# Gated mix of sliding-window attention and a gated GLU: the value product in 64-key halves per two query blocks

## The chip, the cores and the metric

One core of a Trainium2 chip runs the whole kernel. The metric is device time in microseconds (us) of one execution, as the median of several runs. A profiled execution gives, beside it, a trace of every instruction on the five engines: TensorE (PE, with its weight loads listed apart as PEld), VectorE (DVE), ScalarE (ACT), GpSimd (POOL) and SyncE (SP, which issues the DMAs).

## The reference

Both branches read the same input `x` of 2048 tokens by 512 features. The first is causal attention with 32 heads of 16 features and a window of 256 keys; the second is a GLU with 1376 hidden features; a sigmoid gate per token mixes them.

```python
q, k, v = split(x @ wqkv)                     # 32 heads of 16
mask = (i - j >= 0) & (i - j < 256)
p = softmax(where(mask, q @ k.T * 16**-0.5, -1e9))
a = (p @ v) @ wo
b = (sigmoid(x @ w_gate) * (x @ w_up)) @ w_down
g = sigmoid((x * gate_w).sum(-1))
out = g * a + (1 - g) * b
```

## The kernel before, in words

All tokens are cut into 16 blocks of 128, and the heads into 8 groups of 4. One pair of head group and block is a unit; there are 128 (`NU`), and a loop over `u` (lines 593 to 674) works through them with delays. In step `u` the kernel makes the scores of query block `u` with queries in the partitions (`s_part`, line 291), whose row maxima DVE takes (line 307). Nine steps later (`LAG`) it makes the scores again, transposed, with the keys of block `u - 9` in the partitions and up to 384 queries in the columns (`st_part`, line 339). ACT takes their exponential into a tile `pt` in SBUF (line 352) and POOL zeroes what the window excludes (`mask_p`, lines 357 and 362). Each of the two makes four tiles per step, one per head `hh`, in a pair of PSUM buffers of its own: tag `s` and tag `st`, two buffers each. A score matmul uses 64 of the 128 rows of the PE array, so one of `s` and one of `st` run side by side in the two row halves.

In every even step `pv_part` (line 371) multiplies the tiles `pt` of two units, `u - 12` and `u - 11`, with the value rows of their key block. Each head takes 32 columns of the array, so the four heads of a group run side by side on all 128 rows, and each writes 32 partitions of one PSUM bank, `pv`, that holds 512 queries. The products of the three key blocks that a query sees are added up in that bank over three units. As operands are fp32, every matmul is issued as two passes. After each second unit `o_take` (line 391) copies 256 finished queries to SBUF on ACT (line 396), and DVE then clears them in the bank (line 397). The 17th column of every head's value rows is 1, which gives the sums of the softmax.

Around this the PE is filled with projection work: "slots" (`run_slots`, line 573; `turns`, line 519), each with one matmul in either row half, of 512 columns, for the q and k projections (`pj`) and the GLU's gate and up products (`gu`), in three PSUM buffers of tag `misc`. In a step with both score kinds there are three slots behind each head's scores (line 644); in a step with a value product one of them is run right behind it, ahead of the first scores, and two behind these. In steps from 128 on there are no `s` scores, and six slots stand behind each second head. The order of all engines but POOL is the order of the program text; work that may wait is put in the lists `acts` (ACT) and `behind` (DVE), from which one entry is taken per head, and `later` (DMAs, issued at the start of the next step).

DMAs are issued by SP in program order. The row maxima go through DRAM into the tile `ring` (`max_store`, line 324, and `max_load`, line 330): those of query blocks 4s to 4s + 3 are stored at the start of step 4s + 4, loaded in step 4s + 5, and first used by `st_part` in step 4s + 7.

The value rows lie in SBUF in one tile `V` of 16 blocks by 560 floats, and the gate and up products, stored to DRAM, are loaded again into the same memory at the end (`h_load`, line 541): eight places, loads 0 to 4 in steps 130, 132, 134, 136 and 138 (line 669), the rest in the last loop (lines 732 to 782), which multiplies with `w_down` and `wo` in 128-row matmuls. The sigmoid of line 556 takes load 0 in step 138.

Of the kernel before, what the change touches and what calls it, by code (L numbers as in the profile page):

```python
# [7 lines left out]
F32 = mybir.dt.float32  # L8
# [21 lines left out]
VROW = H * VW + 16  # L30
# [17 lines left out]
def gated_mix_kernel(  # L48
# [28 lines left out]
    gu_d = nc.dram_tensor("gu_scratch", (2, NF, P, T), F32, kind="Internal").ap()  # L77
    max_d = nc.dram_tensor("max_scratch", (NG * NC, HG, 2, 4, P), F32, kind="Internal").ap()
# [39 lines left out]
    with ExitStack() as actx:  # L118
# [5 lines left out]
        V = apool.tile([P, NB, VROW], F32, name="V")  # L124
        Vh = V[:, :, 0:H * VW].rearrange("p b (h w) -> p b h w", w=VW)
# [22 lines left out]
        Vf = V.rearrange("p b v -> p (b v)")  # L148
        xraw = Vf[:, NB * VROW - 2 * ND * CH:].rearrange("p (c d t) -> p c d t", c=2, d=ND)
        wvraw = Vf[:, 0:ND * D].rearrange("p (d n) -> p d n", d=ND)  # L150
# [20 lines left out]
        for _ in range(14):  # L171
            mm(warm_ps[:, 0:2 * P], warm[:, 0:P], warm[:, 0:2 * P], start=True, stop=True)
        pv = ps.tile([P, CH], F32, tag="pv", name="pv", bufs=1)
        for k in range(2):
            mm(pv[:, 2 * P * k:2 * P * k + 2 * P], warm[:, 0:P], warm[:, 0:2 * P],
               start=k == 0, stop=True, skip_group_check=True)
# [32 lines left out]
        def fill_v(b0, b1):  # L209
            nc.gpsimd.memset(V[:, b0:b1, H * VW:], 0.0)  # L210
            nc.gpsimd.memset(Vh[:, b0:b1, :, DH:VW], 1.0)
# [5 lines left out]
        def v_part(b, d):  # L217
            if d == 0:
                vp[b] = ps.tile([P, D], F32, tag="misc", name=f"vps{b}", bufs=3)
# [119 lines left out]
        def st_part(u, hh):  # L339
            g, j = divmod(u, NB)  # L340
            if u not in pts:
                pts[u] = ppool.tile([P, HG, 3 * P], F32, tag="pt", name=f"pt{u}", bufs=3)
# [24 lines left out]
        later = []  # L367
        acts = []
        obs = {}

        def pv_part(u):
            g, j = divmod(u, NB)
            p = pts.pop(u)
            last = min(NB, j + 3)
            q = j
            while q < last:
                e = min(last, (q // 4 + 1) * 4)
                for hh in range(HG):
                    h = g * HG + hh
                    mm(  # L380
                        pv[32 * hh:32 * hh + 32, (q % 4) * P:(q % 4 + e - q) * P],
                        V[:, j, h * VW:h * VW + 32],
                        p[:, hh, (q - j) * P:(e - j) * P],
                        start=False, stop=True, skip_group_check=True,
                        tile_position=(0, 32 * hh),
                    )
                q = e
            if j % 2 == 1:
                acts.insert(0, lambda: o_take(g * NC + j // 4, j // 2 % 2))

        def o_take(s, half):
            g, c = divmod(s, NC)
            if half == 0:
                obs[s] = cpool.tile([P, CH], F32, tag="ob", name=f"ob{s}", bufs=2)
            cols = slice(2 * P * half, 2 * P * half + 2 * P)
            nc.scalar.copy(obs[s][:, cols], pv[:, cols])
            behind.insert(0, lambda: nc.vector.memset(pv[:, cols], 0.0))
            if half == 0:
                return
            ob = obs.pop(s)  # L400
# [61 lines left out]
        def gu_mm(f, c, w, k, half=None):  # L462
            fw = width(f, w)
            if (f, c, w) not in gp:
                gp[f, c, w] = ps.tile([P, CH], F32, tag="misc", name=f"gu{f}_{c}_{w}", bufs=3)
            group_mm(gp[f, c, w], fw, gv[:, 0, w, :, 0:fw], gv[:, 1, w, :, 0:fw], c, k, half)
# [72 lines left out]
        hv = Vf[:, 0:16 * CH].rearrange("p (n w t) -> p n w t", w=2, t=CH)  # L539

        def h_load(n):
            c, f = steps[n]
            for w in range(2):
                nc.sync.dma_start(hv[0:FCH[f], n % 8, w], gu_d[w, f, 0:FCH[f], c * CH:(c + 1) * CH])

        def h_skew(n):
            a, b = n + 2, n + 3
            if 0 <= a < len(steps):
                fw = FCH[steps[a][1]]
                hts[a] = cpool.tile([P, CH2], F32R, tag="hb", name=f"hb{a}", bufs=4)  # L550
                src = hv[0:fw, a % 8, 1]
                split(hts[a][0:fw, 0:CH], hts[a][0:fw, CH:], src)
            if 0 <= b < len(steps):
                fw = FCH[steps[b][1]]
                tg, tu = hv[0:fw, b % 8, 0], hv[0:fw, b % 8, 1]
# [31 lines left out]
        HLOAD = N - 2 * AHEAD  # L587
        WD = NU - 5
        done = 0
        slots = turns()  # L590
        sdma = []

        for u in range(N):
            if u == LAG:
                vctx.close()
                ppool = actx.enter_context(tc.tile_pool(name="ppool", bufs=1))
            if u == 4:
# [26 lines left out]
            for hh in range(HG):  # L624
                if hh == 0 and u % 2 == 0:
                    for w in (u - PVLAG - 1, u - PVLAG):
                        if 0 <= w < NU:
                            pv_part(w)
                head = u > PVLAG and hh == 0 and u % 2 == 0
                if head:  # L630
                    run_slots(1)
# [11 lines left out]
                if u >= LAG and (hh < HG - 1 or u % 2 == 0 if u < NU else hh % 2 == 1):  # L643
                    run_slots((GAP if u < NU else 2 * GAP) - (u > PVLAG and u % 2 == 0 and hh == (0 if u < NU else 1)))
# [24 lines left out]
            if u >= HLOAD and (u - HLOAD) % 2 == 0:  # L669
                h_load((u - HLOAD) // 2)  # L670
# [10 lines left out]
        assert not (work or first or going or behind or acts or raw_gu or sdma or pts or obs)  # L681
# [18 lines left out]
        spare = [ppool.tile([P, 3, CH], F32, tag="pt", name=f"spare{k}", bufs=3) for k in range(2)]  # L700
# [31 lines left out]
        for n, (c, f) in enumerate(steps):  # L732
# [39 lines left out]
            for t in range(4):  # L772
# [3 lines left out]
                pa = ps.tile([P, D], F32, tag="misc", name=f"pa{b}", bufs=3)  # L776
# [58 lines left out]
```

## Time and profile before

| | before |
|---|---|
| median of 3 runs | 759.92 us (757.31 to 761.72) |
| span of the profiled execution, first to last instruction | 756.7 us |
| PE busy, share of the span | 748.4 us, 99% |
| DVE, ACT, POOL busy | 480.4, 431.9, 165.8 us |
| matmuls | 6180 |

For the profiled execution itself the span is the time that is listed; it lies 3.2 us under the median of the runs, which also holds what lies around the first and the last instruction. Times inside the trace are us from the start of the span. A PE row gives a matmul's start and a modelled length; since matmuls are pipelined, the cost of one is read from start to next start.

### The profile page before, as it was taken

To read this page: it belongs to the slowest core of one execution; us is meant where nothing else is said; L and a number is where in the kernel's file an instruction comes from. 1 tells how busy PE (TensorE), PEld (TensorE's weight loads), DVE (VectorE), ACT (ScalarE), POOL (GpSimd) and SP (SyncE) were. 2 spreads that over 40 slices of the span, in tenths; PEclk is the share of its full clock that TensorE was granted. 3 is DMA by queue.
4 is the path that set the end of the run, shared out by engine and by line. 5 is a ranking of instruction groups with operands and counts; after the bars stand their busy time and mean duration, and the time that the engine had idled before them with its cause. 6 is when DMAs were issued, how large, how long until landed. Compare 5 with 4: busy or idle time off the path is not lost.

```text
span 756.7 us, 17519 instructions
## 1 busy us (share of the span) xinstructions
PE 748.4 (99%) x6180; PEld 575.8 (76%) x6180; DVE 480.4 (63%) x1459; ACT 431.9 (57%) x930; POOL 165.8 (22%) x256
## 2 busy tenths in 40 slices
PE   8999999999999999999999999999999999999997
PEld 6877777777777777787787777777766778888886
DVE  5346767776776766776677676677512785748381
ACT  5412666666676667666666666656665572616241
POOL 7000233233233233323323223332321000000000
PEclk9999999999999999999999999999999999999999
DMA  8340434426433453444543525443455966557351
GB/s 301 97 112 19 104 101 115 130 68 179 121 105 111 125 149 110 116 111 120 139 125 87 135 73 167 134 116 106 132 177 156 269 221 219 182 190 224 124 151 55
DMA packets 69959, 103.58 MB, mean 137 GB/s; under 512 B 19314, under 2 KB 29042, under 8 KB 69872
## 3 DMA queue, kind: packets, MB, share of 16 engines
q1 hardware_dynamic: 69872, 102.48, 46.0%
q8 instruction: 48, 0.79, 0.4%
q14 instruction: 39, 0.32, 0.2%
HBM read 45.26 MB, written 32.00 MB: 102 GB/s over the span
## 4 chain that ended last, share of the span: by engine, by line
PE 95%; DMA 3%; DVE 1%; ACT 1%; issue 0%; SPq 0%; DVEq 0%; ACTq 0%
PE gu L233 36%; PE pj L233 12%; PE pv L380 11%; PE st L347 6%; PE s L301 6%; PE pd L70 4%; PE pd L72 4%; PE pd L71 4%; PE vps L70 2%; DMA V<-gu_scratch 2%; PE vps L71 2%; PE vps L72 2%; PE pa L72 2%; PE pa L70 2%; PE pa L71 2%; DMA wdraw<-in_wd_dram 1%
## 5 line engine op out<-in xcount | busy, mean ns | idle before, releaser
L307 DVE CUSTOM_DVE_ANT_0 junk<-s,mask 128x384 f32<-128x384 f32 (+2 forms) x512 | 272.0, 531 | 146.8 <-PE st L347 66.4
L233 PE MATMUL gu<-xh,w 64*128 64x512 f32 (+3 forms) x1384 | 359.5, 397 | 0.0
L352 ACT ACTIVATE pt<-st 128x384 f32<-128x384 f32 (+2 forms) x512 | 243.5, 479 | 156.2 <-PE st L347 88.6
L233 PE MATMUL gu<-xl,w 64*128 64x512 f32 (+3 forms) x692 | 245.9, 397 | 0.0
L233 PEld LDWEIGHTS gu<-xh,w 64*128 64x128 f32 (+3 forms) x1384 | 204.5, 183 | 34.8 <-issue 10.5
L357 POOL TENSOR_SCALAR_AFFINE_SELECT pt<-pt 128x512 f32<-128x512 f32 x128 | 85.3, 666 | 392.1 <-ACT pt L352 392.1
L347 PE MATMUL st<-ring 64*128 64x384 f32 (+2 forms) x536 | 163.3, 317 | 0.0
L301 PE MATMUL s<-ring 64*128 64x384 f32 (+2 forms) x536 | 159.5, 320 | 0.0
L233 PEld LDWEIGHTS gu<-xl,w 64*128 64x128 f32 (+3 forms) x692 | 124.2, 183 | 13.2 <-issue 6.4
L347 PEld LDWEIGHTS st<-ring 64*128 64x128 f32 x536 | 97.2, 184 | 11.1 <-ACT pt L352 1.5
L301 PEld LDWEIGHTS s<-ring 64*128 64x128 f32 x536 | 94.8, 184 | 10.6 <-issue 2.9
L233 PE MATMUL pj<-xh,wqh 64*128 64x512 f32 (+1 forms) x232 | 95.4, 414 | 1.3 <-ACT xh L66 1.3
L233 PE MATMUL pj<-xl,wqh 64*128 64x512 f32 (+1 forms) x232 | 92.1, 400 | 0.0
L380 PE MATMUL pv<-pt,V 128*32 128x384 f32 (+2 forms) x1408 | 91.0, 388 | 0.0
L233 PE MATMUL pj<-xh,wql 64*128 64x512 f32 (+1 forms) x232 | 74.2, 398 | 0.0
L362 POOL TENSOR_SCALAR_AFFINE_SELECT pt<-pt 128x512 f32<-128x512 f32 x112 | 70.9, 633 | 0.0
L70 PE MATMUL pd<-ring,hb 128*128 128x512 f32 (+1 forms) x176 | 69.6, 395 | 1.3 <-ACT hb L66 1.3
L72 PE MATMUL pd<-ring,hb 128*128 128x512 f32 (+1 forms) x176 | 69.2, 393 | 0.2
L71 PE MATMUL pd<-ring,hb 128*128 128x512 f32 (+1 forms) x176 | 68.6, 390 | 0.4 <-DVE ring L111 0.4
L380 PEld LDWEIGHTS pv<-pt,V 128*32 128x32 f32 x1408 | 37.2, 109 | 35.9 <-issue 29.4
L471 ACT COPY sp<-gu 128x512 f32<-128x512 f32 (+2 forms) x88 | 51.4, 585 | 21.1 <-PE gu L233 19.7
L66 ACT CAST hb<-V 128x512 fp32r<-128x512 f32 (+1 forms) x44 | 27.3, 620 | 54.5 <-DVE V L557 54.2
(74 smaller groups left out, 904.4 us busy)
## 6 DMA issues: line engine op xcount, KB each, us to landing
gu_scratch<-sp SPq DMA_DIRECT2D x80, 256.0 KB
V<-gu_scratch SPq DMA_DIRECT2D x80, 256.0 KB
ring<-sh SPq DMA_DIRECT2D x128, 128.0 KB
ring<-sl SPq DMA_DIRECT2D x64, 128.0 KB
guraw<-in_wgu_dram SPq DMA_DIRECT2D x20, 256.0 KB
V<-in_xT_dram SPq DMA_DIRECT2D x16, 256.0 KB
oT_scratch<-ob SPq DMA_DIRECT2D x128, 32.0 KB
xl<-oT_scratch SPq DMA_DIRECT2D x16, 256.0 KB
```

The source lines that it names most:

```text
L70: mm(ps, lh, rh, start=first, stop=False)
L71: mm(ps, lh, rl, start=False, stop=False)
L72: mm(ps, ll, rh, start=False, stop=last)
L233: mm(pt[0:fw], (wl if w == 2 else wh)[r, d], (xl if w == 1 else xh)[r, d, c * CH:(c + 1) * CH], start=k == 0 and half != 1, stop=k == 3 * ...
L301: mm(pt[:, (k - k0) * P:(e - k0) * P], lhsT, blk(g, k, hh, 1, e - k), start=k == k0, stop=e == i + 1, skip_group_check=True,)
L307: nc.vector.tensor_tensor_reduce(junk[:, 0:n], pt[:, 0:n], mask[:, 3 * P - n:], scale=1.0, scalar=NEG, op0=ALU.add, op1=ALU.max, accum_out ...
L347: mm(pt[:, (q - j) * P:(e - j) * P], lhsT, blk(g, q, hh, 0, e - q), start=q == j, stop=e == last, skip_group_check=True,)
L352: nc.scalar.activation(pts[u][:, hh, 0:n], pt[:, 0:n], AF.Exp, scale=SCALE)
L357: nc.gpsimd.affine_select(p[:, :, 0:P], p[:, :, 0:P], pattern=[[0, HG], [1, P]], compare_op=ALU.is_ge, fill=0.0, base=0, channel_multiplie ...
L362: nc.gpsimd.affine_select(p[:, :, 2 * P:], p[:, :, 2 * P:], pattern=[[0, HG], [-1, P]], compare_op=ALU.is_gt, fill=0.0, base=0, channel_mu ...
L380: mm(pv[32 * hh:32 * hh + 32, (q % 4) * P:(q % 4 + e - q) * P], V[:, j, h * VW:h * VW + 32], p[:, hh, (q - j) * P:(e - j) * P], start=Fals ...
L471: nc.scalar.copy(t[0:width(f, w)], gp.pop((f, c, w))[0:width(f, w)])
```

## The change

The value product now goes by queries in place of keys. `pv_burst` computes, in the same even steps, the whole output of two query blocks `i` and `i + 1` of a head group at once, from the tiles `pt` of the key blocks `i - 2` to `i + 1`. Each key block is cut in two halves of 64 keys; one half is seen by 64 + 256 = 320 queries. The halves with even `k` run in the upper 64 rows of the array, those with odd `k` in the lower, each head in its 32 columns: eight tiles of 64 rows by 32 columns. Rows of the array that are apart must write different PSUM banks, so there are two sums, `acc[0]` and `acc[1]`, taken for the burst from the buffers of `s` and of `st`. `o_take` follows at once: ACT copies `acc[0]` to SBUF, DVE adds `acc[1]` to it. The bank `pv` and its clearing go; `misc` has four buffers.

A value row tile is no longer read in place. Every block of `V` is stored to DRAM (`v_d`) and the 68 columns of a head group are loaded from there as `vg` (`v_load`, one DMA of 16 x 128 rows of 272 bytes), at step 10 and then at steps 16, 32, ... The freed memory, `region`, holds seven tiles `pt`, and at the end seven places for `h_load`, whose loads 0 to 4 move to steps 135, 136, 137, 137 and 138.

```diff
-            if j % 2 == 1:
-                acts.insert(0, lambda: o_take(g * NC + j // 4, j // 2 % 2))
...
-            nc.scalar.copy(obs[s][:, cols], pv[:, cols])
-            behind.insert(0, lambda: nc.vector.memset(pv[:, cols], 0.0))
...
+        def v_load(g):
+            nc.sync.dma_start(
+                vg[g % 2][:, 0:NB * GW].rearrange("p (b w) -> p b w", w=GW),
+                v_d[:, :, g * GW:(g + 1) * GW].rearrange("b p w -> p b w"),
+            )
+
+        def pv_burst(u, n):
+            g, i = divmod(u, NB)
+            acc = [
+                ps.tile([P, CH], F32, tag=tag, name=f"pv{tag}{u}", bufs=2) for tag in ("s", "st")
+            ]
+            span = {
+                k: (max(0, 64 * k), min(n * P, 64 * k + 5 * 64))
+                for k in range(-4, 2 * n) if i + k // 2 >= 0
+            }
+            order = [
+                sorted((k for k in span if k % 2 == half), key=lambda k: (span[k][0] - span[k][1], k))
+                for half in range(2)
+            ]
+            for m in range(len(order[0])):
+                for hh in range(HG):
+                    for half in range(2):
+                        k = order[half][m]
+                        j = i + k // 2
+                        q0, q1 = span[k]
+                        o = -(k // 2) * P
+                        r = slice(64 * half, 64 * half + 64)
+                        c = j * GW + hh * VW
+                        mm(
+                            acc[half][32 * hh:32 * hh + 32, q0:q1],
+                            vg[g % 2][r, c:c + 32], pts[g * NB + j][r, hh, q0 + o:q1 + o],
+                            start=m == 0, stop=m == len(order[0]) - 1, skip_group_check=True,
+                            tile_position=(64 * half, 32 * hh),
+                        )
+            o_take(g, i, n, acc)
+
+        def o_take(g, i, n, acc):
...
+            nc.scalar.copy(part, acc[0][:, 0:n * P])
+            nc.vector.tensor_tensor(part[:, lo:], acc[1][:, lo:n * P], part[:, lo:], op=ALU.add)
...
-                pj[s] = ps.tile([P, CH], F32, tag="misc", name=f"pj{s}", bufs=3)
+                pj[s] = ps.tile([P, CH], F32, tag="misc", name=f"pj{s}", bufs=4)
...
+                later.append((v_d[b], V[:, b]))
...
-        HLOAD = N - 2 * AHEAD
+        HLOAD = {N - 5: [0], N - 4: [1], N - 3: [2, 3], N - 2: [4]}
...
+            if u == LAG + 1 or u % NB == 0 and 0 < u < NU:
+                v_load(u // NB)
...
-                    for w in (u - PVLAG - 1, u - PVLAG):
-                        if 0 <= w < NU:
-                            pv_part(w)
+                    if u in bursts:
+                        pv_burst(*bursts[u])
```

## Rows read from the trace of the kernel before

**Rows 1.** The page: busy time by engine, and the chain by engine.
```profile
PE 748.4 (99%) x6180; PEld 575.8 (76%) x6180; DVE 480.4 (63%) x1459; ACT 431.9 (57%) x930; POOL 165.8 (22%) x256
...
PE 95%; DMA 3%; DVE 1%; ACT 1%; issue 0%; SPq 0%; DVEq 0%; ACTq 0%
```

**Rows 2.** Timeline of PE, 304 to 307 us: start, length, line, out<-in, shape, count.
```profile
304.49 1.50 PE L380 MATMUL pv<-pt,V 128*32 128x384 f32 x16
305.92 0.50 PE L233 MATMUL pj<-xh,wqh 64*128 64x512 f32 x1
...
306.26 0.33 PE L347 MATMUL st<-ring 64*128 64x384 f32 x1
...
306.90 0.33 PE L347 MATMUL st<-ring 64*128 64x384 f32 x1
```

**Rows 3.** Timeline of PE, a value product of eight passes, at 312 us.
```profile
312.39 1.51 PE L380 MATMUL pv<-pt,V 128*32 128x256 f32 x32
313.83 0.50 PE L233 MATMUL gu<-xl,w 64*128 64x512 f32 x1
```

**Rows 4.** Groups by form: busy us, mean ns; idle before.
```profile
L307 DVE CUSTOM_DVE_ANT_0 junk<-s,mask 128x256 f32<-128x256 f32 x32 | 13.6, 425 | 14.6 <-PE st L347 10.5 <-PE s L301 3.7
```

**Rows 5.** Timeline of all engines around the last value product, 579 us.
```profile
578.28 0.86 PE L380 MATMUL pv<-pt,V 128*32 128x256 f32 x16
...
579.07 0.47 PE L233 MATMUL gu<-xh,w 128*96 128x512 f32 x1
...
579.25 0.37 ACT L396 COPY ob<-pv 128x256 f32<-128x256 f32 x1 [0.24 <-PE pv L380]
...
579.75 0.27 DVE L397 MEMSET pv<- 128x256 f32 x1 [4.02 <-ACT ob L396]
```

**Rows 6.** Timeline of all engines, 598 to 600.6 us.
```profile
598.51 0.62 ACT L66 CAST xh<-woraw 128x512 fp32r<-128x512 f32 x1 [5.76 <-DMA woraw<-in_wo_dram]
...
599.16 0.69 DVE L67 TENSOR_TENSOR xl<-woraw,xh 128x512 fp32r<-128x512 f32 x1 [1.00 <-ACT xh L66]
...
599.76 0.68 DVE L67 TENSOR_TENSOR hb<-V,hb 128x512 fp32r<-128x512 f32 x1
...
600.50 0.51 PE L72 MATMUL pd<-ring,hb 128*128 128x512 f32 x1
```

**Rows 7.** Timeline of PE around a late slot, 97 to 99 us.
```profile
97.72 0.33 PE L347 MATMUL st<-ring 64*128 64x384 f32 x1
...
98.00 0.49 PE L233 MATMUL gu<-xh,w 64*128 64x512 f32 x1
...
98.34 0.62 PE L233 MATMUL gu<-xh,w 64*128 64x512 f32 x2
```

**Rows 8.** Waits of PEld: us in total, times, longest.
```profile
PEld gu L233 <- ACT pr L245: 1.9, 6, 0.3
```

**Rows 9.** Timeline of PE, step 130.
```profile
548.65 0.37 PE L347 MATMUL st<-ring 64*128 64x384 f32 x2
```

**Rows 10.** Timeline of DVE at the start of the value product of rows 2.
```profile
304.42 0.08 DVE L307 DVE_READ_ACCUMULATOR2_ANT mx<- 128x1 f32 x1
```

**Rows 11.** Timelines of SP (step 16 on) and of PE (step 19).
```profile
103.37 1.70 SPq L328 DMA_DIRECT2D max_scratch<-nt  x4
...
108.56 0.56 SPq L333 DMA_DIRECT2D ring<-max_scratch  x1
...
114.37 0.34 PE L347 MATMUL st<-ring 64*128 64x384 f32 x1
```

**Rows 12.** The page: DMA queues (packets, MB, share of 16 engines).
```profile
q1 hardware_dynamic: 69872, 102.48, 46.0%
```

**Rows 13.** Timelines of SP (step 136) and of ACT (step 138).
```profile
572.49 0.82 SPq L544 DMA_DIRECT2D V<-gu_scratch  x2
...
580.94 0.63 ACT L556 ACTIVATE V<-V 128x512 f32<-128x512 f32 x1
```

More of the change, by code (lines that the diff above doesn't have):

```diff
@@ L29 @@
 VW = DH + 1
-VROW = H * VW + 16
+VROW = H * VW
+GW = HG * VW
+PR = 7
+PW = HG * 3 * P
+REGION = PR * PW
+NHV = 7
+HV0 = REGION - NHV * 2 * CH
+BURST = 2
 SCALE = DH ** -0.5
@@ L170, in gated_mix_kernel @@
         warm_ps = ps.tile([P, CH], F32, tag="st", name="warm_ps", bufs=2)
-        for _ in range(14):
+        for _ in range(16):
             mm(warm_ps[:, 0:2 * P], warm[:, 0:P], warm[:, 0:2 * P], start=True, stop=True)
[L173 to L176, printed above, removed]
         raw_q = load_wqk(0)
@@ L218, in v_part @@
             if d == 0:
-                vp[b] = ps.tile([P, D], F32, tag="misc", name=f"vps{b}", bufs=3)
+                vp[b] = ps.tile([P, D], F32, tag="misc", name=f"vps{b}", bufs=4)
             bs = slice(b * P, (b + 1) * P)
@@ L399, in o_take @@
+        def o_take(g, i, n, acc):
+            s = g * NC + i // 4
+            if i % 4 == 0:
+                obs[s] = cpool.tile([P, CH], F32, tag="ob", name=f"ob{s}", bufs=2)
+            part = obs[s][:, i % 4 * P:(i % 4 + n) * P]
+            lo = 64 if i == 0 else 0
+            nc.scalar.copy(part, acc[0][:, 0:n * P])
+            nc.vector.tensor_tensor(part[:, lo:], acc[1][:, lo:n * P], part[:, lo:], op=ALU.add)
+            if (i + n) % 4:
                 return
-            ob = obs.pop(s)
+            ob, c = obs.pop(s), i // 4
@@ L590, in gated_mix_kernel @@
         slots = turns()
+        bursts = {}
+        w = 0
+        while w < NU:
+            n = BURST if w + 8 < NU else 2
+            bursts[w + n - 1 + PVLAG] = w, n
+            w += n
         sdma = []
@@ L596, in gated_mix_kernel @@
                 ppool = actx.enter_context(tc.tile_pool(name="ppool", bufs=1))
+                for k in range(2):
+                    vg.append(ppool.tile([P, NB * GW + 16], F32, name=f"vg{k}"))
+                    nc.gpsimd.memset(vg[k][:, NB * GW:], 0.0)
+            if u == LAG + 1 or u % NB == 0 and 0 < u < NU:
+                v_load(u // NB)
             if u == 4:
@@ L625, in gated_mix_kernel @@
                 if hh == 0 and u % 2 == 0:
-                    for w in (u - PVLAG - 1, u - PVLAG):
-                        if 0 <= w < NU:
-                            pv_part(w)
-                head = u > PVLAG and hh == 0 and u % 2 == 0
-                if head:
-                    run_slots(1)
+                    if u in bursts:
+                        pv_burst(*bursts[u])
+                if hh == 0:
+                    head = min(2, bursts.get(u, (0, 0))[1] // 2)
+                    run_slots(head)
                 if u < NU:
@@ L643, in gated_mix_kernel @@
                 if u >= LAG and (hh < HG - 1 or u % 2 == 0 if u < NU else hh % 2 == 1):
-                    run_slots((GAP if u < NU else 2 * GAP) - (u > PVLAG and u % 2 == 0 and hh == (0 if u < NU else 1)))
+                    run_slots((GAP if u < NU else 2 * GAP) - (hh < head if u < NU else head * (hh == 1)))
             if u < LAG - 1:
@@ L668, in gated_mix_kernel @@
                 behind.append(lambda c=(u - SUMS) // 4: later.append(sums_invert(c)))
-            if u >= HLOAD and (u - HLOAD) % 2 == 0:
-                h_load((u - HLOAD) // 2)
+            for n in HLOAD.get(u, ()):
+                h_load(n)
             if u >= N - 2:
@@ L680, in gated_mix_kernel @@
         nc.sync.dma_start(gsum, gu_d[0, NF - 1, FCH[NF - 1]].rearrange("(b p) -> p b", p=P))
-        assert not (work or first or going or behind or acts or raw_gu or sdma or pts or obs)
+        assert not (work or first or going or behind or acts or raw_gu or sdma or obs)
         def slot(h, d, c):
@@ L699, in gated_mix_kernel @@
         o_raw = [blocks(free_slot(1, k, 2)) for k in range(2)]
-        spare = [ppool.tile([P, 3, CH], F32, tag="pt", name=f"spare{k}", bufs=3) for k in range(2)]
+        spare = [
+            region[:, 3 * CH * k:3 * CH * (k + 1)].rearrange("p (n t) -> p n t", t=CH) for k in range(2)
+        ]
         wide = [blocks(spare[k][:, 2]) for k in range(2)]
@@ L775, in gated_mix_kernel @@
                 nc.scalar.activation(acc, pd[t], AF.Copy, scale=omg[:, b:b + 1])
-                pa = ps.tile([P, D], F32, tag="misc", name=f"pa{b}", bufs=3)
+                pa = ps.tile([P, D], F32, tag="misc", name=f"pa{b}", bufs=4)
                 for d in range(ND):
```

49 lines of the change are left out of this document (15 added, 34 removed).

## The prediction, made before the changed kernel was run

> **What bounds the kernel now.** I read the page first: PE is busy for 99% of the span and holds 95% of the chain that ended last, DVE and ACT are busy for about 60% [rows 1]. So PE's stream of matmuls is the bound, and a change counts by what it takes from that stream or by a wait that it puts in. Next comes the timeline of PE around a value product, read from start to start: the product starts at 304.49, the first slot behind it at 305.92, the first scores at 306.26, the second pair of scores at 306.90 [rows 2]. From first to second scores stand 384 + 512 + 512 columns in 0.64 us, 0.45 ns a column: 0.17 us for a score pair, 0.23 us for a slot. The stream has almost no gaps; the one that recurs is a slot waiting for ACT, six times [rows 7, 8].
>
> **The value product itself.** Before, a product of two units streams 768 columns per head, all heads side by side: 1.43 us in four passes, 1.44 us in eight shorter ones [rows 2, 3]; the last one of a group, 384 columns, takes 0.79 us [rows 5]. So 384 columns cost 0.64 us, 1.67 ns a column, and 0.15 to 0.16 us is fixed (draining the array, the first weights). That the passes double in number adds only 0.01 us. A head group has four products of 1.43, three of 1.44 and one of 0.79: 10.8 us.
>
> After, each row half streams 64 + 128 + 192 + 256 = 640 columns, the two halves side by side: 1.07 us plus 0.16. Eight tiles start one after another where there were four, so I take 1.25. The first product of a group has only its own keys: the longer half has 384 columns, 0.81 us. A group takes 0.81 + 7 x 1.25 = 9.6 us. That is 1.27 less, **10.2 us less** over eight groups. Bounds: 11.4 with nothing for the extra tiles; 4.4 if a pass of 64 columns takes no less than one of 128 (0.11 us).
>
> One rule speaks against the shorter passes. TensorEngine Tiling (Array Packing) of the Trainium skill, section Instruction Overhead, gives each matmul some 60 cycles of overhead, an estimated 25 ns per pass; a group goes from 44 passes to 60, so by the rule the gain would be about 3 us smaller. The two products of 768 columns [rows 2, 3] put the cost of an extra pass at a tenth of that, and the sum goes by them.
>
> **The wait that it adds.** The two sums occupy one buffer of `s` and one of `st`. Right behind the product PE runs a slot, the first scores (other buffers), two slots and the second scores, which need both buffers back; they are due 0.98 us after that first slot starts [rows 2]. The way back: ACT's copy starts 0.18 us after the slot's start and lasts 0.37 [rows 5], to 0.55. DVE starts 0.03 us after an ACT result [rows 6], or 0.13 [rows 5]. The add has no row; the nearest is DVE's two-input operation on 256 columns from PSUM, 0.42 us [rows 4]. That gives 1.00, and PE follows DVE by 0.06 [rows 6]: the `st` buffer is free at 1.06 us (1.16 with the slower start), 0.08 (0.18) late.
>
> What lateness costs is shown by a slot that waits for ACT: the scores at 97.72 should be followed 0.17 later, the slot came at 98.00, 0.11 late, and the next at 98.34, 0.11 more than a slot takes, since the weights behind the wait were not loaded ahead [rows 7]. So a wait costs its lateness plus 0.11: here 0.19 us, in the 58 products of steps 12 to 126: **11 us more**. Bounds: nothing if the add is back 0.11 us before it is due, which needs a chain 0.19 us quicker; 17 us with the slower start. Queued behind the waiting score matmul are all later slots and scores, hence the whole loop.
>
> In steps 128 to 136 no `s` scores and no slots stand between: both first `st` matmuls run together right behind the slot [rows 9], so the second is due at 0.34 and waits for 1.06: 0.72 + 0.11, five times, **4.2 us more** (3 to 4.7).
>
> **Smaller terms.** The product also needs its buffers before it starts. DVE finishes the row maxima of the buffer in question at 304.50, and with 0.06 to PE that is 0.07 after the start of 304.49 [rows 2, 10]; this is so in twelve steps, where DVE had projection work just before: 0.8 us more (0 to 2). The fourth `misc` buffer removes the six waits of rows 8 at 0.21 each: 1.3 less. The clearing on DVE (0.27 us, rows 5) gives way to the add (0.42); DVE has a third of the span free, but the add delays the first row maxima, whose buffer is due only two heads later: nothing beyond the wait above.
>
> SP gets 16 stores and eight loads, about half a microsecond each, and is not the bound. Loading the first `vg` in step 10 for step 12 leaves some 8 us; by bytes against all the traffic that DMA takes 1.9 us, by packets 10.2 (2048 of them, at 80 ns a packet over 16 engines) [rows 12]. I take 4, as its packets are a fifth of the mean in size: 0.3 us of wait (0 to 4). `h_load` 0 moves from step 130 to 135, about 4 us ahead of the issue at 572.49 of step 136 and so some 12 ahead of its use at 580.94 [rows 13]; that hides it, and loads 1 to 4 follow before their turns: nothing (0 to 3 if the queues are full). POOL's two small clears stand beside other work.
>
> **Sum.** -10.2 + 11.0 + 4.2 + 0.8 - 1.3 + 0.3 = **+4.8 us**. The profiled span of 756.7 becomes 761.5; the median of the runs lies 3.2 above the span, so 764.7, say **764.5 us**, 0.6% slower than 759.9. A difference of 0.5% (3.8 us) is about what a measurement of this kernel can tell from none.
>
> **Rivals.**
> *The sums are back in time.* If the add is short, or DVE sees ACT's result sooner, the wait of the loop vanishes and only part of the tail's stays: 764.5 - 11 - 1, **752.5 us**, faster. It decides at 0.87 us from the first slot. For it: the chain hangs on one operation without a row; against it: every link has its measured length. In between, half the wait leaves 758.
>
> *The value loads hold up the row maxima.* In steps 16, 32, ... 112 `v_load` is issued ahead of `max_store`, in the same queue. From that store at 103.37 to the scores that need the loaded maxima at 114.37 are 11 us, with two small DMAs in them, of which the first lands within 3.5 us (the load behind it is issued at 108.56) [rows 11]. Counting 2 us for each landing, a `v_load` of up to about 4.7 us is hidden; at 6 us each costs 1.3, seven times: **773 us**, slower; at the upper bound of 10.2 it would be 38 over the forecast. For it: rows of 272 bytes; against it: all three bounds but the last lie below. DMA: Bandwidth & Descriptors of the Trainium skill, Specifications, says that transfers under 512 bytes are done as read-modify-write; an estimate of twice the 4 us puts it past that point, and by this rule the time would be some 787.
>
> *The row halves do not overlap for these tiles.* Score pairs and slots start together in both halves [rows 2] and four heads together in columns, but no row has both at once. In turn, each product would take 1.07 more (the first 0.43): 63 us, **828 us**.
>
> *The change of tiling no longer drains.* The row split now stays at 64 between slots and product. If that spared the fixed 0.15 and the 0.11 of the first slot, 16 us would go: **748 us**. Against it: behind the product at 579 only the columns change (128x32 to 128x96), and its 0.79 us hold the fixed part too [rows 5].
>
> **How the numbers follow.** The forecast has a chance of 0.58: about 0.31 over 763.7, 0.26 within 0.5%, 0.01 below. The sums in time: 0.20, faster but for 0.03. The value loads: 0.12, slower but for 0.02. No overlap: 0.04, slower. No drain: 0.03, faster. The rest, 0.03, one each. Together faster 0.22, same 0.32, slower 0.46. The range of 751 to 774 takes in the sums in time and the milder case of the loads; no overlap, no drain and loads beyond it stay outside.
>
> **What would show it.** From start to start the product should take about 1.25 us, and 0.8 in the first of a group. The second scores should stand some 1.06 us behind the first slot in place of 0.98, with the weight load waiting for DVE's add, and the next slot 0.11 late. PE's waits for ACT at line 245 should be gone, and a DVE add of about 0.42 us should follow each ACT copy. The forecast is wrong if the second scores start at 0.98, if the product takes 2 us, or if PE waits on the row maxima in steps 19, 35, ...

## The result, and the profile after

The changed kernel takes **768.67 us** (median of 4 runs, 767.32 to 769.50) against 760.13 of the kernel before beside it: a ratio of 1.0114, 95% interval 1.0091 to 1.0137. The forecast was 764.5 with a range of 751 to 774, and "slower" had the largest chance. The profiled span grew by 11.1, from 756.7 to 767.8; 1.6 of that stand ahead of the first scores (they start at 40.99 instead of 39.38), where PE, behind waits of 0.90 and 0.23 us for its first operands, ran for some 7 us at the lower of its two clock levels (1.2 instead of 2.4 GHz; the granted clock was 0.52 from 10 to 15 us, and 1.00 there in the trace of before). In the profiles of the runs below the first scores start anywhere between 38.6 and 41.5, so I count these 1.6 us to the one execution and not to the change.

From the page after (busy time, chain by engine, DMA queue), to be read against [rows 1, 12]:
```profile
PE 753.6 (98%) x8612; PEld 648.8 (85%) x8612; DVE 491.2 (64%) x1459; ACT 445.0 (58%) x930; POOL 166.5 (22%) x256
...
PE 92%; DMA 4%; DVE 2%; SPq 1%; issue 1%; ACT 1%; POOL 0%; DVEq 0%; ACTq 0%; POOLq 0%
...
q1 hardware_dynamic: 88688, 111.39, 49.5%
```
PE is still the bound, but it is now idle for 14.2 us of the span where it was idle for 8.3, and DVE's share of the chain is 2% where it was 1%.

The timeline around the same product as in [rows 2], all engines (start, length, engine, line, out<-in, shape, count, idle before):
```profile
308.96 0.37 PE L405 MATMUL pvs<-region,vg 64*32 64x256 f32 x1
308.97 0.40 PE L405 MATMUL pvst<-region,vg 64*32 64x256 f32 x1
...
309.94 0.22 PE L405 MATMUL pvs<-region,vg 64*32 64x64 f32 x1
...
310.09 0.22 PE L405 MATMUL pvs<-region,vg 64*32 64x64 f32 x1
310.11 0.22 PE L405 MATMUL pvst<-region,vg 64*32 64x64 f32 x1
...
310.25 0.50 PE L238 MATMUL pj<-xh,wqh 64*128 64x512 f32 x1
...
310.38 0.37 ACT L419 COPY ob<-pvs 128x256 f32<-128x256 f32 x1 [0.85 <-PE pvst L405]
310.59 0.33 PE L306 MATMUL s<-ring 64*128 64x384 f32 x1
...
310.79 0.42 DVE L420 TENSOR_TENSOR ob<-pvst,ob 128x256 f32<-128x256 f32 x1 [0.22 <-DMA ring<-sh]
...
311.24 0.33 PE L306 MATMUL s<-ring 64*128 64x384 f32 x1
311.27 0.18 PEld L353 LDWEIGHTS st<-ring 64*128 64x128 f32 x1
311.27 0.44 PE L353 MATMUL st<-ring 64*128 64x384 f32 x1
...
311.55 0.39 PE L238 MATMUL pj<-xh,wql 64*128 64x512 f32 x1
```
The two row halves do run side by side (308.96 and 308.97). From start to start the product takes 1.29 us (most take 1.30) where it took 1.43. Then the wait: the slot starts at 310.25, ACT's copy 0.13 later, DVE's addition ends at 311.21, and the second `st` scores start 0.06 behind that, at 311.27: 1.02 us behind the slot instead of 0.98. Their weights are loaded only then (the PEld row at 311.27; before, they had been loaded 0.23 ahead of the scores), and the next slot in their row half follows 0.28 behind them, at 311.55; between the same two it is 0.18 in e1_own_bank below (303.69 and 303.87), where nothing waits.

PE's waits in the changed kernel (in all, times, longest), the first from the weight loads, the others from the matmuls:
```profile
PEld st L353 <- DVE ob L420: 10.0, 20, 1.1
...
PE st L353 <- DVE ob L420: 3.7, 7, 0.9
PE pd L77 <- ACT hb L73: 2.6, 2, 2.1
```
The waits for ACT's `pr` [rows 8] are gone. These lists hold only the gaps that the profile can see; most waits of 0.04 us don't show as such. So I summed starts: for each of the 58 products of steps 12 to 126, from the first product row to the first slot behind it, and from there to the next product, in both traces. **The products take 7.05 us less, and the stretches between them 12.5 more.** A usual stretch is 0.14 longer. Two kinds are longer by more: behind the first product of a head group (0.42 to 0.46, but for the very first), and in steps 32, 64 and 96 (0.95 to 0.99); so are three single ones (0.46, 0.36 and 0.48 in steps 20, 36 and 104). Step 64, DVE and PE:
```profile
292.88 0.69 DVE L479 TENSOR_TENSOR w<-guraw,w 128x512 fp32r<-128x512 f32 x1
293.48 0.61 DVE L322 TENSOR_SCALAR nm<-mx 128x16 fp32r<-128x16 f32 x1
...
293.71 0.50 PE L238 MATMUL pj<-xh,wqh 64*128 64x512 f32 x1
...
294.13 0.55 DVE L323 SCALAR_TENSOR_TENSOR nm<-mx,nm 128x16 fp32r<-128x16 f32 x1
...
295.01 0.42 DVE L420 TENSOR_TENSOR ob<-pvst,ob 128x256 f32<-128x256 f32 x1
...
295.49 0.44 PE L353 MATMUL st<-ring 64*128 64x384 f32 x1 [0.57 <-DVE ob L420]
```
A weight split and the split of the row maxima stand ahead of the addition in DVE's queue. The addition starts 1.30 us behind the slot of 293.71 instead of 0.54, and the scores come 1.78 behind that slot. Behind the first product of a group it is the split of the row maxima that stands ahead of it (in step 60 it starts 0.88 behind its slot).

The rest: the five products of steps 128 to 136 take 0.6 less and the stretches behind them 2.3 more; the last product of all, 384 columns before [rows 5], takes 0.5 more; from the first down projection to the end it is 1.7 more. Together -7.05 + 12.5 - 0.6 + 2.3 + 0.5 + 1.7 = +9.4 us, with the 1.6 of the start the 11 between the spans; between the medians it is 8.5.

### The profile page after: what moved, and what is told of

It is laid out like the page before. It is cut to its first block, busy times and chain, and to the rows that moved or that the text cites. A ratio compares the mean times of both kernels' runs of the same rounds, so it can differ in the third digit from the quotient of the medians.

```text
span 767.8 us, 22658 instructions
## 1 busy us (share of the span) xinstructions
PE 753.6 (98%) x8612; PEld 648.8 (85%) x8612; DVE 491.2 (64%) x1459; ACT 445.0 (58%) x930; POOL 166.5 (22%) x256
## 4 chain that ended last, share of the span: by engine, by line
PE 92%; DMA 4%; DVE 2%; SPq 1%; issue 1%; ACT 1%; POOL 0%; DVEq 0%; ACTq 0%; POOLq 0%
PE gu L238 33%; PE pj L238 13%; PE pvs L405 8%; PE s L306 6%; PE st L353 5%; PE pd L79 4%; PE pd L77 4%; PE pd L78 4%; DMA region<-gu_scratch 2%; PE vps L77 2%; PE pvst L405 2%; PE vps L78 2%; PE vps L79 2%; PE pa L77 2%; PE pa L79 2%; PE pa L78 2%
## 5 line engine op out<-in xcount | busy, mean ns | idle before, releaser
L358 ACT ACTIVATE region<-st 128x384 f32<-128x384 f32 (+2 forms) x512 | 241.1, 474 | 120.7 <-PE st L353 60.3
L238 PE MATMUL gu<-xl,w 64*128 64x512 f32 (+3 forms) x692 | 238.2, 396 | 0.0
L238 PEld LDWEIGHTS gu<-xh,w 64*128 64x128 f32 (+3 forms) x1384 | 208.3, 183 | 7.8 <-issue 0.6
L353 PE MATMUL st<-ring 64*128 64x384 f32 (+2 forms) x536 | 171.1, 329 | 4.3 <-DVE ob L420 3.7
L363 POOL TENSOR_SCALAR_AFFINE_SELECT region<-region 128x512 f32<-128x512 f32 x128 | 86.1, 673 | 358.4 <-ACT region L358 328.0
L238 PEld LDWEIGHTS gu<-xl,w 64*128 64x128 f32 (+3 forms) x692 | 115.5, 183 | 3.0
L405 PEld LDWEIGHTS pvs<-region,vg 64*32 64x32 f32 x1920 | 63.4, 106 | 25.3 <-issue 18.3
L405 PE MATMUL pvs<-region,vg 64*32 64x256 f32 (+3 forms) x1920 | 82.7, 302 | 0.1
L405 PE MATMUL pvst<-region,vg 64*32 64x192 f32 (+3 forms) x1920 | 81.7, 299 | 0.0
L420 DVE TENSOR_TENSOR ob<-pvst,ob 128x256 f32<-128x256 f32 (+1 forms) x64 | 26.6, 416 | 74.2 <-PE pj L238 27.9
L368 POOL TENSOR_SCALAR_AFFINE_SELECT region<-region 128x512 f32<-128x512 f32 x112 | 71.0, 634 | 0.0
```

Source lines behind the costliest of these rows:

```text
L238: mm(pt[0:fw], (wl if w == 2 else wh)[r, d], (xl if w == 1 else xh)[r, d, c * CH:(c + 1) * CH], start=k == 0 and half != 1, stop=k == 3 * ...
L353: mm(pt[:, (q - j) * P:(e - j) * P], lhsT, blk(g, q, hh, 0, e - q), start=q == j, stop=e == last, skip_group_check=True,)
L363: nc.gpsimd.affine_select(p[:, :, 0:P], p[:, :, 0:P], pattern=[[0, HG], [1, P]], compare_op=ALU.is_ge, fill=0.0, base=0, channel_multiplie ...
L368: nc.gpsimd.affine_select(p[:, :, 2 * P:], p[:, :, 2 * P:], pattern=[[0, HG], [-1, P]], compare_op=ALU.is_gt, fill=0.0, base=0, channel_mu ...
L405: mm(acc[half][32 * hh:32 * hh + 32, q0:q1], vg[g % 2][r, c:c + 32], pts[g * NB + j][r, hh, q0 + o:q1 + o], start=m == 0, stop=m == len(or ...
L420: nc.vector.tensor_tensor(part[:, lo:], acc[1][:, lo:n * P], part[:, lo:], op=ALU.add)
```

## The experiments

"After" is the changed kernel. Each ratio is to the kernel before, run on the same chip beside it (759.5 to 760.1 us there). Where I speak of "between products" it is the same sum as above, steps 12 to 126, against the kernel before.

| run | median us | ratio (95% interval) | products | between |
|---|---|---|---|---|
| after | 768.67 | 1.0114 (1.0091 to 1.0137) | -7.05 | +12.5 |
| e1_own_bank | 755.62 | 0.9940 (0.9917 to 0.9963) | -7.07 | +2.5 |
| e2_slot_moved | 762.06 | 1.0030 (1.0016 to 1.0045) | -7.10 | +6.5 |
| e3_add_pieces | 782.90 | 1.0301 (1.0277 to 1.0326) | -7.07 | +25.9 |
| e4_late_loads | 761.60 | 1.0022 (1.0009 to 1.0036) | 0.0 | 0.0 |
| e5_pass_order | 761.08 | 1.0017 (1.0004 to 1.0031) | -1.92 | +2.0 |
| e6_four_blocks | 770.98 | 1.0151 (1.0136 to 1.0167) | see text | see text |
| e7_v_twice | 773.68 | 1.0188 (1.0168 to 1.0208) | -6.40 | +13.1 |
| e8_four_order | 772.40 | 1.0174 (1.0158 to 1.0190) | see text | see text |
| e9_copy_from_st | 755.76 | 0.9946 (0.9926 to 0.9966) | -6.95 | +1.6 |
| e10_three_misc | 767.12 | 1.0093 (1.0075 to 1.0111) | -7.01 | +12.5 |
| e11_later_add | 753.03 | 0.9909 (0.9894 to 0.9925) | -6.94 | -1.4 |

### e1_own_bank: is it the wait for the addition?

```
-    ps.tile([P, CH], F32, tag=tag, name=f"pv{tag}{u}", bufs=2) for tag in ("s", "st")
+    ps.tile([P, CH], F32, tag=tag, name=f"pv{tag}{u}", bufs=n_buf)
+    for tag, n_buf in (("s", 2), ("pv", 1))
...
-    tag="misc", bufs=4
+    tag="misc", bufs=3
```


> The changed kernel, but the second partial sum has a PSUM bank of its own (one buffer), so no second score waits any more for DVE's addition; the first sum still takes a bank of the first scores, and the 'misc' bank is given up again (3 instead of 4 buffers). The product's passes and the tiles stay as they are. Theory A (most of the loss is the wait of the second scores on the addition, 58 products at about .17 us plus the larger ones, 12.5 us between steps 12 and 126 and 2.3 us at steps 128 to 136): about 12 to 14 us come back, less 1.3 us for the copies that the fourth 'misc' buffer hid: 756 us (753 to 760), and the 20 waits of PE's weight load on the addition are gone from the trace. Theory B (the loss comes from what else changed, the value rows' loads, more DMA traffic, a lower clock): within 2 us of the changed kernel's 768.7 us.

Measured: 755.62 us, 13.0 less than after, as theory A had it. The stretches between products fall from +12.5 to +2.5, those of steps 128 to 136 from +2.3 to -0.1. The same place as above, in this run:
```profile
302.72 0.50 PE L238 MATMUL pj<-xh,wqh 64*128 64x512 f32 x1
...
303.26 0.42 DVE L420 TENSOR_TENSOR ob<-pvpv,ob 128x256 f32<-128x256 f32 x1 [0.29 <-DMA ring<-sh]
...
303.69 0.34 PE L353 MATMUL st<-ring 64*128 64x384 f32 x1
303.70 0.34 PE L306 MATMUL s<-ring 64*128 64x384 f32 x1
```
The addition stands where it stood, 0.54 behind the slot, and still ends only just ahead of the scores; but these no longer need its bank and start 0.97 behind the slot, both halves together. So 10.0 of the 12.5 us go with the wait for DVE's addition. (The run also has three `misc` buffers; e10_three_misc shows that these change nothing.) Of the 2.5 that are left, most stand at the start of a product, ahead of its addition:
```profile
270.09 0.33 PE L306 MATMUL s<-ring 64*128 64x384 f32 x1
...
270.29 0.08 DVE L312 DVE_READ_ACCUMULATOR2_ANT mx<- 128x1 f32 x1
...
270.52 0.37 PE L405 MATMUL pvs<-region,vg 64*32 64x256 f32 x1
```
The product of step 60 stands 0.43 behind the last scores; before it was 0.26. Its first sum takes a bank of `s`, which DVE reads until 270.37. This is so in the twelve products of steps 20, 28, ... 100 and 124: 0.15 to 0.17 each, 0.31 in step 20, 2.0 us in all. In after the same twelve lose 0.02 to 0.04 each, 0.14 in step 20, 0.5 in all: PE comes later there, and the bank is nearly free.

### e2_slot_moved and e3_add_pieces: what does being late cost?

```
-    run_slots((GAP if u < NU else 2 * GAP) - (hh < head if u < NU else head * (hh == 1)))
+    run_slots((GAP if u < NU else 2 * GAP) - head * (hh == 1))
```


> The changed kernel, with one slot of other work moved: in steps with a product all GAP slots stand behind the first head's scores, and one fewer behind the second head's, so that the second scores are issued about .23 us later. Nothing else changes; the banks and the addition stay. Theory A (PE is late by about .03 us for the addition, and loses .11 us more for want of weights loaded ahead): the addition is done when the second scores come, the typical .15 us per product vanishes for some 56 products, 7 to 10 us: about 760 us (757 to 763); the steps where DVE is busy with other work (12 mod 16, and 32, 64, 96) keep part of theirs. Theory B (the loss after a product is not this wait): 768 us, unchanged within 1.5 us.

```
-    nc.vector.tensor_tensor(part[:, lo:], acc[1][:, lo:n * P], part[:, lo:], op=ALU.add)
+    for q in range(lo, n * P, 64):
+        nc.vector.tensor_tensor(part[:, q:q + 64], acc[1][:, q:q + 64], part[:, q:q + 64], op=ALU.add)
```


> The changed kernel with DVE's addition cut into four pieces of 64 columns, which takes the bank about .2 us later from the second scores (four short instructions instead of one of .42 us). Theory A (the end of the addition is what PE waits for after each product): every .1 us that it ends later is paid at once by PE, about .2 us for 63 products, +9 to +16 us: about 781 us (776 to 786). Theory B (the addition is hidden): 0 to 2 us, 769 to 771 us.

Measured: 762.06 and 782.90, both within their theory A. The same place in the run with the slot moved:
```profile
306.88 0.50 PE L238 MATMUL pj<-xh,wqh 64*128 64x512 f32 x1
...
307.41 0.42 DVE L420 TENSOR_TENSOR ob<-pvst,ob 128x256 f32<-128x256 f32 x1 [0.28 <-DMA ring<-sh]
...
308.08 0.33 PE L306 MATMUL s<-ring 64*128 64x384 f32 x1
308.08 0.33 PE L353 MATMUL st<-ring 64*128 64x384 f32 x1
```
and in the run with the addition in pieces:
```profile
314.49 0.50 PE L238 MATMUL pj<-xh,wqh 64*128 64x512 f32 x1
...
315.02 0.62 DVE L421 TENSOR_TENSOR ob<-pvst,ob 128x64 f32<-128x64 f32 x4 [0.23 <-PE gu L238]
...
315.47 0.33 PE L306 MATMUL s<-ring 64*128 64x384 f32 x1
315.79 0.41 PE L353 MATMUL st<-ring 64*128 64x384 f32 x1
```
With the slot moved, the addition ends at 307.83 and the scores come at 308.08: nothing is late, and the stretch behind this product is as long as before (6.456 against 6.472). In pieces, the addition takes 0.62 instead of 0.42, and the `st` scores start 1.30 behind the slot instead of 1.02; this stretch is 0.39 longer than before, where after has 0.14. So 0.28 us more delay cost 0.25, nearly one for one, while the first 0.04 us cost 0.14: this wait costs some 0.10 on top, as much as the next slot of its row half is late behind it (0.28 instead of 0.18 above). That this is for the weights, which were not loaded ahead, fits the rows; no run changes it alone. The larger waits where DVE has other work ahead (steps 32, 64, 96) are hardly moved by a slot: +0.8 is left of +0.95.

### e4_late_loads: the stretch at the end

```
-    HLOAD = N - 2 * AHEAD
+    HLOAD = {N - 5: [0], N - 4: [1], N - 3: [2, 3], N - 2: [4]}
...
-    if u >= HLOAD and (u - HLOAD) % 2 == 0:
-        h_load((u - HLOAD) // 2)
+    for n in HLOAD.get(u, ()):
+        h_load(n)
```


> The kernel before, with one part of the change alone: the first five loads of the hidden rows are issued at N-5 to N-2 instead of every second step from N-10. Theory A (the bunched loads cost the 1.7 us by which the stretch from the first down projection to the end is longer in the changed kernel): +1 to +2.5 us over the kernel before, and the wait of the down projection on ACT's hb stands in its trace with about 2 us. Theory B (those 1.7 us come from elsewhere, as the place of the hidden rows in the shared region): 0 (within .6 us).

Measured: 761.60, a ratio of 1.0022, which is 1.6 us (0.7 to 2.7). In its profile the part from the first down projection to the end is 1.0 us longer than before, and all stretches between products are the same to 0.01 us. PE's wait for `hb` in it (before: 1.3 in two waits):
```profile
PE pd L70 <- ACT hb L66: 2.0, 1, 2.0
```
By the times the edit costs what the end lost. But this part of the program is not steady: with the same late loads it was 0.1 us shorter than before in the profile of e1_own_bank, and 3.1 longer in that of e9_copy_from_st. The size of the term, 1 to 2 us, therefore rests on the times.

### e5_pass_order: why 1.30 us and not 1.25?

On e1_own_bank:
```
+    order = [[v[0], v[-1], *v[1:-1]] for v in order]
```


> As the run with the second sum in a bank of its own (755.6 us), with one edit: in each row half the passes go 256, 64, 192, 128 columns instead of 256, 192, 128, 64. Theory A (the product is 1.30 us and not the forecast 1.25 because its last passes of 64 columns are over sooner than eight tiles can be issued again, so tiles stand idle at the end): the narrow pass is issued behind a wide one, the product falls to about 1.25 us, 55 products by .05 us: 752.8 us (751 to 754). Theory B (the .05 us are at the start of the product, where the array changes its tiles, or are the clock's): product still 1.30 us, 755.6 us, unchanged within 1 us.

Measured: 761.08, 5.5 us *slower* than e1_own_bank. Neither theory: the product does not fall to 1.25 nor stay, it rises to 1.406 (5.7 us over the 56 products that have such a pass). PE's rows in its product of step 16, which starts at 102.09:
```profile
102.52 0.21 PE L406 MATMUL pvs<-region,vg 64*32 64x64 f32 x1
...
102.74 0.34 PE L406 MATMUL pvs<-region,vg 64*32 64x192 f32 x1
...
102.76 0.34 PE L406 MATMUL pvpv<-region,vg 64*32 64x192 f32 x1
...
103.23 0.27 PE L406 MATMUL pvs<-region,vg 64*32 64x128 f32 x1
103.25 0.27 PE L406 MATMUL pvpv<-region,vg 64*32 64x128 f32 x1
103.27 0.27 PE L406 MATMUL pvs<-region,vg 64*32 64x128 f32 x1
103.28 0.27 PE L406 MATMUL pvpv<-region,vg 64*32 64x128 f32 x1
```
What theory A said of the cause fits these rows, what it said of the cure does not. In the first passes of after the tiles start 7 ns apart; behind a pass of 64 columns they start 17 ns apart, eight tiles in some 0.13 us, while 64 columns last 0.05 (a pass of 256 follows the last in 0.215). So a narrow pass is bound by the starts of its tiles. And the tiles never close up again: the 192 and the 128 columns behind it start 17 ns apart as well, to the last one at 103.28, which then has 128 columns to go instead of 64. With the narrow pass at the end, as in the change, only the end itself is stretched. The first product of a group bears this out: its longer half ends with 128 columns, and it takes 0.17 besides its columns (0.81 less 0.64), the others 0.23. Descending widths are the better of the two orders.

### e6_four_blocks and e8_four_order: a larger product

On e1_own_bank, and the second with the pass order of e5 besides:
```
-BURST = 2
+BURST = 4
```


> As the run with the second sum in a bank of its own (755.6 us), with one edit: BURST = 4, so that 30 of the products take four query blocks (passes of up to 320 columns) and 34 products stand for 64. Theory A (a product has a fixed price besides its columns, 1.30 us against 1.07 us of columns): 30 fixed prices of .2 us vanish, 5 to 8 us: about 749 us (747 to 752), product of four blocks about 2.35 us in the trace. Theory B (the drain of twice the width, ACT's copy some .6 us and DVE's addition some .8 us, takes the gain back in waits of the next scores): a wait of PE on the copy or on DVE's row maxima of .2 to .3 us per product, 755 to 760 us.

> Both edits together on the bank of its own: four query blocks to a product and the narrowest pass second. Theory A (fixed price and end of the product are separate and both real): the gain of four blocks, 5 to 8 us, and .05 us for each of 34 products, 1.7 us: 747.5 us (745 to 751), faster than the kernel before by some 12 us. Theory B (the waits of the next scores take the difference): no better than the better of the two single edits.

Measured: 770.98 and 772.40; theory B in both, and worse than B's numbers. In e6_four_blocks the products are what A said: 2.376 us for four blocks, 72.5 us for all of them against 79.3 in e1_own_bank. But what stands outside them, from the first scores to the first down projection, grows from 461.2 to 483.9 us. Its timeline:
```profile
319.89 0.50 PE L238 MATMUL gu<-xl,w 64*128 64x512 f32 x1
...
320.02 0.59 ACT L419 COPY ob<-pvs 128x512 f32<-128x512 f32 x1 [1.87 <-PE pvpv L405]
...
320.64 0.69 DVE L420 TENSOR_TENSOR ob<-pvpv,ob 128x512 f32<-128x512 f32 x1 [2.25 <-ACT ob L419]
...
321.25 0.55 DVE L312 CUSTOM_DVE_ANT_0 junk<-s,mask 128x384 f32<-128x384 f32 x1
...
321.86 0.18 PEld L306 LDWEIGHTS s<-ring 64*128 64x128 f32 x1 [0.39 <-DVE mx L312]
```
and its largest wait of the weight loads:
```profile
PEld s L306 <- DVE mx L312: 44.8, 100, 1.3
```
The addition of twice the width holds DVE for 0.69 us, the first row maxima behind it start only at 321.25, and the third head's `s` scores wait for their bank: 100 such waits (10 in e1_own_bank). DVE is busy for 63% of the span here as before, and still does not catch up within the step. The edit of e5 adds 0.106 to a product here too (2.482).

### e7_v_twice: the value rows' way through DRAM

```
 v_load(u // NB)
+v_load(u // NB)
```


> The changed kernel, with each load of a group's value rows issued twice. Theory A (the value rows' way through DRAM is off the path, as the forecast had it): 768.7 us, unchanged within 1.5 us. Theory B (rival of the forecast: the value rows' load stands in SP's queue and in the transfers ahead of the row maxima and holds the scores of a new group up): 7 more loads at 1 to 2 us each where a group begins, 776 to 783 us, with a wait of PE on a DMA at steps 16, 32, ... 112.

Measured: 773.68, between the two. PE's and SP's waits in it:
```profile
PE pvs L405 <- DMA vg<-v_scratch: 3.0, 1, 3.0
```
```profile
SPq L378 <- DMA vg<-v_scratch: 31.9, 8, 4.8
```
The second load of each pair holds SP until the first has landed, 4.0 us on average: that is the time of one load, counted from the end of its issue (the forecast took 4). At the head of the very first group the second copy comes 3.0 us late for the first product, which accounts for most of the 5 us. At the other seven groups SP is held up by some 4 us ahead of the store of the row maxima, and PE has no wait for it: the stretches of steps 16, 32, ... 112 sum to +3.72, and to +3.71 in after. The rival is refuted, and a single load costs nothing; only the first has slack of less than a second one.

### e10_three_misc: the fourth buffer

```
-    tag="misc", bufs=4
+    tag="misc", bufs=3
```


> The changed kernel with 3 instead of 4 'misc' buffers, one PSUM bank left empty. Theory A (the forecast's term: the fourth buffer hides ACT's copies that the gate and up products waited for before, 1.9 us in 6 waits): +1.0 to +2 us, about 770 us, and the waits of the products' weights on ACT's pr are back. Theory B (those waits went because the products stand elsewhere now, as in the run with a bank of its own, where 3 buffers show none of them): 768.7 us, unchanged within .7 us.

Measured: 767.12, 1.5 less than after, with intervals that overlap; the sums of the table are nearly the same, and no wait for `pr` comes back. Theory B.

### e9_copy_from_st and e11_later_add: what e1_own_bank still lost

On e1_own_bank:
```
-    for tag, n_buf in (("s", 2), ("pv", 1))
+    for tag, n_buf in (("st", 2), ("pv", 1))
```


> As the run with the second sum in a bank of its own (755.6 us), with one edit: the first sum takes its bank from the second scores' pool instead of the first scores'. Theory A (what that run still loses after some products, 2.5 us between steps 12 and 126, are first scores that stand one bank short behind DVE's row maxima, 3.3 us in 10 waits of PE's weight load): these waits vanish, and the second scores don't wait, since ACT's copy is done some .5 us behind the product and they come 1.0 us behind it: 753 us (751.5 to 754.5). Theory B (ACT is late instead, its exponentials and the copy share one queue): the second scores wait for the copy, 756 to 760 us.

And on this:
```
-    nc.vector.tensor_tensor(part[:, lo:], acc[1][:, lo:n * P], part[:, lo:], op=ALU.add)
+    def rest_of_it():
+        nc.vector.tensor_tensor(part[:, lo:], acc[1][:, lo:n * P], part[:, lo:], op=ALU.add)
...
+    acts.append(lambda: behind.append(rest_of_it))
```


> As the run with the first sum in the second scores' pool and the second in a bank of its own (755.8 us), with one edit: DVE's addition is no longer issued right behind ACT's copy but one to two heads later, behind the first row maxima of its step (nothing waits for its bank for two steps). Theory A (what that run still loses after products, 1.6 us between steps 12 and 126, is first scores that wait for row maxima standing behind the addition in DVE's queue, 6.7 us in 20 waits): most of these waits vanish, 754 us (753 to 755.5), and the stretch between products is within .5 us of the kernel before in sum. Theory B (DVE has a backlog at these places with or without the addition): the waits and the time stay, 755.8 us within 1 us.

Measured: 755.76 and 753.03. With the bank from `st` alone, the 0.16 us that e1_own_bank lost in steps 2 and 10 of a group go (1.16 and 0.93 us in sum, now 0.01 and 0.00); they are the late starts of the products behind these steps, which were shown above. But others come: behind the first product of a group +1.3 in sum. And steps 32, 64 and 96 keep some 0.4 each (0.3 to 0.4 in e1_own_bank). The second scores wait for ACT's copy, as theory B has it, only in steps 130 to 136 (1.2 us in four waits). The waits for the row maxima in this run, of the weight loads and of the matmuls:
```profile
PEld s L306 <- DVE mx L312: 6.2, 17, 0.7
```
```profile
PE s L306 <- DVE mx L312: 0.5, 3, 0.2
```
So the edit took away one kind of wait for the row maxima and brought another. With the addition issued later the second row is gone and the first is what it is in the kernel before:
```profile
PEld s L306 <- DVE mx L312: 0.6, 2, 0.4
```
The stretches are now 1.4 us *shorter* than before in sum (7 times 0.2 in steps 14 of a group, where the kernel before waited for ACT, six times for `pr`, and within 0.04 elsewhere). From e9_copy_from_st to e11_later_add that is 3.1 us for the place of one addition in DVE's queue. This version beats both kernels: 0.9% less than the kernel before, 15.6 us less than the changed one.

## Why the prediction was right, and where its terms were off

**Right in direction and in mechanism.** The row halves overlap, the product keeps a fixed part besides its columns (0.23 us), PE stays the bound, and the gain in the products is more than eaten by a wait for DVE's addition, through the buffer of `st`; that of `s` is free with ACT's copy. The chain of the forecast is found link by link: ACT 0.13 behind the slot (0.18 forecast), 0.37, DVE 0.04 behind it, 0.42, PE 0.06: 1.02 instead of 1.06 us. There is luck in this: the addition had no row, and its stand-in, another operation, happened to last as long; and the scores are only 0.04 late. By the figures above (0.04, and 0.10 on top) a chain some 0.14 us shorter would have cost nothing, an estimate.

**The product** gains 7.1 us over all 64 (7.05 and 0.6, less 0.5 in the last), not 10.2. The step that failed is "Eight tiles start one after another where there were four, so I take 1.25": it is 1.30, since the last passes of 64 columns are bound by the starts of their tiles. The bound of 4.4 (4.2 by the prediction's own figures) was the right thought, a narrow pass that costs more than its columns. The step that set the rule aside, "the sum goes by" the two products of 768 columns, was an extrapolation past 128 columns, the narrowest pass in them. TensorEngine Tiling (Array Packing) of the Trainium skill, Instruction Overhead, would have given a gain of some 7 us, an estimate near the measured one; the runs still speak against an overhead per matmul, since the same passes in another order cost 0.106 more (e5_pass_order), and a four-block product of 96 matmuls has only 0.01 more besides its columns than a two-block one of 64 (2.376 less 2.133 against 1.300 less 1.067).

**The wait in the loop** was put at 11.0 and is 10.0 by e1_own_bank, but put together otherwise. The usual one costs 0.14, not 0.19. What was missed is the queue on DVE: the forecast held that the add delays the row maxima by "nothing beyond the wait above", and that nothing delays the add. In steps 32, 64, 96 and behind the first product of a group DVE's other work does; the larger waits make up some 5 us beyond 0.14 each, so that the total comes near the forecast is luck in part. And once the addition's own wait is gone, the addition costs 3.1 us through the row maxima (e9_copy_from_st against e11_later_add).

**The tail** was 2.3 to 2.4 us, not 4.2: against e1_own_bank the wait costs 0.6 to 0.8 behind three of the five products, but only 0.15 and 0.18 in steps 130 and 132, where 0.83 each was forecast. The waits themselves are there (0.7 to 1.1 us in the weight loads of steps 128 to 134); what makes up for them in those two steps is open. **The product's own buffers**, forecast 0.8 in twelve steps, cost 0.5 in after, and in the very twelve; in e1_own_bank, where the wait behind the product no longer hides it, the term is 2.0, as each late start costs 0.16 and not 0.07. (Eight products take 1.32 to 1.35 instead of 1.30, in every run with the same passes, whichever bank they use; why is open.) **The fourth `misc` buffer**, forecast 1.3 less, gives nothing (e10_three_misc): the waits of [rows 8] went with 3 buffers as well. Their size was right (seven stretches of e11_later_add are 0.2 shorter), their cause was not. What removed them was not tried; ACT's copy of the product has moved from a later place to right behind the product. **The first `v_load`**, forecast 0.3, costs nothing: one load lands in 4.0 us, inside its slack. DMA: Bandwidth & Descriptors of the Trainium skill, Specifications, has rows under 512 bytes done as read-modify-write; the prediction's estimate from it, twice the 4 us and a kernel of 787, did not come. Whether a part of the 4.0 is due to that, no run shows. **The later `h_load`s**, forecast "nothing (0 to 3 if the queues are full)", cost 1 to 2 us.

By the sum, +9.4 stands where +4.8 was forecast: 3.1 less gain in the product, 1.7 more in the loop (12.5 for 11.0 + 0.8 - 1.3 + 0.3) and 1.7 at the end, against 1.9 less in the tail. The median is 4.2 above the forecast.

## What to carry to other kernels

When an accumulator borrows a buffer of a tight loop, the time to hand it back counts from the last matmul through every engine that empties it, and the loop paid nearly every overrun in full, with some 0.10 us on top of each wait; a bank of its own, with the emptying pushed behind the work that others wait for, made a loss of 1.1% a gain of 0.9%. Ask of an engine with a third of its time free what stands ahead of the new operation in its queue at that moment, not what its average is. With small tiles side by side, put the wide passes first and the narrow ones last: that was the better of the two orders tried here.

## What the runs showed of the hardware that was not expected

Tiles of 64 rows by 32 columns start 7 ns apart in the first passes of a product, and 17 ns apart behind a pass of 64 columns, and that spacing then stays to the end of the product: the same passes took 1.30 us in descending order and 1.406 with the narrow one second. A wait of 0.04 us cost PE 0.14, one of 0.28 more only 0.25 more. Four additions of 64 columns took DVE 0.62 us where one of 256 took 0.42.
